# Attention with a memory and a gated expert on one core: products of ones at the start, beta spread by TensorE, a scaling pass folded, second score products of 64 rows

## The chip, the cores and the metric

The kernel runs on one core of a Trainium2 chip. The metric is the device time of one execution in microseconds, as the median of several runs; lower is better. Engines are named as in the profile: PE is TensorE, PEld its loading of weights, DVE is VectorE, ACT is ScalarE, POOL is GpSimd, SP is SyncE, which issues nearly all transfers here.

## The reference

There are 4 batches, 8 heads, 576 positions and 64 features a head. Each head has causal attention and a retrieval from a memory matrix; a gate made of beta mixes the two; a gated expert follows over all 2304 positions of width 512, with 1536 hidden columns.

```python
scores = scale * np.matmul(q, k.transpose(0, 1, 3, 2))
scores = np.where(causal, -1000000000.0, scores)
a = np.exp(scores - scores.max(-1, keepdims=True))
a /= a.sum(-1, keepdims=True) + 1e-09
local = np.matmul(a, v)
mem_ret = np.einsum('bhsd,bhde->bhse', q_p, M_prev)
mem_norm = np.einsum('bhsd,bhd->bhs', q_p, z_prev)[..., None] + 1e-06
g = 1.0 / (1.0 + np.exp(-beta))[None, :, None, None]
attn = g * mem_ret / mem_norm + (1 - g) * local
x = attn.transpose(0, 2, 1, 3).reshape(B * S, H * D)
out = ((1 / (1 + np.exp(-(x @ w_gate)))) * (x @ w_val)) @ w_out
```

Here q_p is phi(q), which is q + 1 for positive q and exp(q) otherwise.

## The kernel before

**Work and stages.** The 2304 rows are cut into six groups of 384: four groups hold the first 384 positions of a batch, two tail groups hold the last 192 positions of two batches each. The first group that is run is a tail group, the last one too. A group has four pairs of heads (24 pairs in all, numbered n from 0). A pair has three chunks c of 128 queries; each chunk gives scores for two heads j, which lie in the two halves of the 128 partitions. In a group of 384 the three chunks see 128, 256 and 384 keys. In a tail group two chunks see 512 keys, and the third, with 64 rows of either batch, sees 576 in two parts. After a chunk's scores VectorE adds the mask and finds the row's extreme (`scores`, L597), ScalarE takes the exponential (L606), the result is turned (`turn`) and multiplied with the values (`values`), scaled by `scaled`, and added to the memory's part (`memory`, scaled too). `scaled` divides by the sum in column D of the product and multiplies with the gate: gs for the memory, ga for the attention, both made by `gates` from beta.

**The expert.** `moe` goes over 12 blocks of 128 hidden columns for each group. Its products (L315) are of the type fp32r, which takes one pass; each is made of three products of a high and a low part. The weights come as 64-bit numbers and are turned into high and low parts in the first group (`convert`).

**Two forms of scores.** For n below 9 (SPLIT), and for the 64-row chunks, `heads` (L560) multiplies plain fp32: for each head a product over 64 rows, the two heads in the two halves of the array. Its profile rows say 64\*128, or 64\*64 for the 64-row chunks, and a plain fp32 product is recorded as two parts. From n = 9 on, `split` makes tiles for fp32r: `kq`, whose 128 partitions hold the high part of one head's queries and keys and the low part of its keys beside another copy of the queries' high part, and `ql`, the low part of its queries. The score of one head is then a product over all of kq and a second one of ql with kq, both of 128 rows; half of ql is zero (`half` writes the zeros once, on GpSimd), so that the unwanted half of kq adds nothing.

**Order.** Every operation is recorded in `Program` with an engine, a cost, and what it reads and writes; `plan` orders the operations of each engine by their recorded places and by these costs, and `issue` tries 800 shifted variants of the order, judged by its own model, and emits the best. So a changed cost or a removed operation can move any row of any engine. PE, DVE, ACT, POOL and SP each run their rows in this order and wait at a row until what it needs is there. In the model a product before the time COLD counts one and a half times.

**Beta.** It is loaded by one transfer that repeats its 8 numbers on all 128 partitions, behind the first keys and a memory matrix on SP. The first products of the program are the first pair's `heads`, once the first kp tile is there.

Of the kernel before, what the change touches and what calls it, by code (L numbers as in the profile page):

```python
# [9 lines left out]
F32 = mybir.dt.float32  # L10
# [19 lines left out]

WHEN = (20, 36)

COLD = 8.0

START = 0.7

# [204 lines left out]
def tile_attention_memory_moe(  # L241
# [82 lines left out]
    def act(n, emit, r, w):  # L324
        pg.add("act", 0.09 + n / 1200.0, emit, r, w)
# [22 lines left out]
    idn = sb.tile([128, 128], F32, name="idn")  # L348
    mask = sb.tile([128, 512], F32, name="mask")
    mask2 = sb.tile([128, 256], F32, name="mask2")  # L350
    bt = sb.tile([128, H], F32, name="bt")
    gs = sb.tile([128, H], F32, name="gs")
    ga = sb.tile([128, H], F32, name="ga")

# [19 lines left out]
            ), ["mask2"], ["mask2"])  # L374

    def gates():
        act(H, lambda: nc.scalar.activation(out=bt, in_=bt, func=AF.Exp, scale=-1.0), ["bt"], ["bt"])
        dve(H, lambda: nc.vector.tensor_scalar(
            out=gs, in0=bt, scalar1=1.0, scalar2=None, op0=ALU.add), ["bt"], ["gs"])
        dve(H * 8, lambda: nc.vector.reciprocal(out=gs, in_=gs), ["gs"], ["gs"])  # L380
        dve(H, lambda: nc.vector.tensor_scalar(
            out=ga, in0=gs, scalar1=-1.0, scalar2=1.0, op0=ALU.mult, op1=ALU.add), ["gs"], ["ga"])

    def half(t, k):
        r = slice(64, 128) if k[1] == 0 else slice(0, 64)
        pool(GT, lambda: nc.gpsimd.memset(t[r].bitcast(F32), 0.0), [], [k + ("z",)], fast=True)

    def pad(t, k):
        pool(64, lambda: nc.gpsimd.memset(t[:, S:], 0.0), [], [k + ("pad",)])
# [17 lines left out]
    plain, turned = {"wide": 4 * DM, 0: None}, {"wide": 4 * DM, 1: None}  # L407
    kq_r = Ring("kq", [128, 2 * GT], F32R, 5,
                {0: (in_wr, "wr", 2), **{i + 1: (in_wt, "wt", i) for i in range(4)}})
    ql_r = Ring("ql", [128, GT], F32R, 2, init=half)  # L410
    a_r = Ring("a", [128, 640], F32, 6, init=pad)
    st_r = Ring("st", [128, 2], F32, 6)
    at_r = Ring("at", [128, 1280], F32, 4)
# [84 lines left out]
    def scaled(out, out_k, t, tk, ring, eps, gate, gate_k):  # L498

        r, rk = ring.take()  # L500
        dve(6, lambda: nc.vector.tensor_scalar(
            out=r, in0=t[:, :, :, D], scalar1=eps, scalar2=None, op0=ALU.add), [tk], [rk])
        dve(48, lambda: nc.vector.reciprocal(out=r, in_=r), [rk], [rk])
        tt(nc.vector, ALU.mult, r, r, gate.unsqueeze(1).to_broadcast([128, 3, 2]), 6, [rk, gate_k], [rk])
        tt(nc.vector, ALU.mult, out, t[:, :, :, :D], r.unsqueeze(3).to_broadcast([128, 3, 2, D]), GT,
           [tk, rk], out_k)

# [24 lines left out]
    def split(n):  # L532


        if n >= NP or n < SPLIT:
            return
        u = pairs[n]
        u.kq = [[], []]
        ql = [ql_r.take() for _ in range(2)]
        nq, nk = (128, 512) if u.tail else (GT, GT)  # L540
        qs, ks = slice(u.qa, u.qa + nq), slice(u.ka, u.ka + nk)
        used = slice(0, S + nq if u.tail else 2 * GT)
        for e, (kp, kk) in enumerate(u.kp):
            for j in range(2):
                kq, k = kq_r.take()
                h, l = slice(64 * j, 64 * j + 64), slice(64 - 64 * j, 128 - 64 * j)
                kh, kd, kl, kx = k + ("h",), k + ("d",), k + ("l",), ql[j][1] + (e,)
                copy(kq[h, used], kp[h, used], used.stop, [kk], [kh])
                copy(kq[l, qs], kp[h, qs], nq, [kk], [kd])
                sub(nc.vector, kq[l, ks], kp[h, ks], kq[h, ks].bitcast(F32), nk, [kk, kh], [kl])  # L550
                q = ql[j][0][:, e * nq:(e + 1) * nq]
                sub(nc.vector, q[h], kp[h, qs], kq[h, qs].bitcast(F32), nq, [kk, kh], [kx])
                u.kq[j].append((kq, [kh, kd, kl], q, [kx, ql[j][1] + ("z",)]))

    def heads(u, es, sp, js, k0, k1):

        for e, q, m0, m1 in es:
            kp, _ = u.kp[e]
            for j, r in enumerate(js):
                nc.tensor.matmul(  # L560
                    out=sp[j][0][m0:m1, :k1 - k0], lhsT=kp[r, u.qa + q:u.qa + q + m1 - m0],
                    rhs=kp[r, u.ka + k0:u.ka + k1], start=True, stop=True)

    def scores(n, c):

        u = pairs[n]
        q0, W = items_of(u.g)[c]
        pair = u.tail and c == 2
        js = [slice(64 * j, 64 * j + 64) for j in range(2)]
        if (n, c) == (HP, 0):  # L570
            a_r.n, a_r.at = 5, 0
        a = [a_r.take() for _ in js]
        st = [st_r.take() for _ in js]
        ns = [(0, 320), (320, W)] if pair else [(0, W)]
        def part(i, k0, k1):
            m = k1 - k0
            sp = [bank("att") for _ in js]
            if pair:
                es = [(0, 128, 0, 64), (1, 128, 64, 128)]
                mk, mk_k = (mask2[:, :m], "mask2") if i else (mask[:, :m], "mask")  # L580
            else:
                es = [(c if u.tail else 0, q0, 0, 128)]
                mk, mk_k = mask[:, 512 - W:], "mask"
            with pg.block():
                if n < SPLIT or pair:
                    pe(4 * m / 2385.0 + 0.3, lambda: heads(u, es, sp, js, k0, k1),
                       [u.kp[e][1] for e, *_ in es], [sp[j][1] for j in range(2)])
                for j in range(2) if n >= SPLIT and not pair else ():
                    for e, q, m1 in [(es[0][0], q0, 128)]:
                        kq, kk, ql, kx = u.kq[j][e]  # L590
                        keys = kq[:, u.ka + k0:u.ka + k1]
                        out, out_k = sp[j][0][:m1, :m], sp[j][1]
                        matmul(out, kq[:, u.qa + q:u.qa + q + m1], keys, m, kk, [out_k], True, False)
                        matmul(out, ql[:, q:q + m1], keys, m, kk + kx, [out_k], False, True)
            for j in range(2):
                (aj, ak), (sj, sk), (pj, pk) = a[j], st[j], sp[j]
                dve(m + 60, lambda aj=aj, sj=sj, pj=pj: nc.vector.tensor_tensor_reduce(  # L597
                    out=aj[:, k0:k1], in0=pj[:, :m], in1=mk, scale=-0.125,
                    scalar=3.0e38 if i == 0 else sj[:, i - 1:i],
                    op0=ALU.add, op1=ALU.min, accum_out=sj[:, i:i + 1],  # L600
                ), [pk, mk_k] + [sk] * (i > 0), [ak, sk])

        for i, (k0, k1) in enumerate(ns):
            part(i, k0, k1)
        for (aj, ak), (sj, sk) in zip(a, st):
            act(W + 120, lambda aj=aj, sj=sj: nc.scalar.activation(  # L606
                out=aj[:, :W], in_=aj[:, :W], func=AF.Exp, scale=-1.0, bias=sj[:, len(ns) - 1:len(ns)],
            ), [ak, sk], [ak])
        u.a[c] = a
# [107 lines left out]
    def attn():  # L717
# [3 lines left out]
        load_pair(1)  # L721
        feature(0)
        load_values(0)
        load(bt, beta.unsqueeze(0).to_broadcast([128, H]), 500, [], ["bt"])
        pg.part = "attention"
        load_values(1)
        late = []
# [167 lines left out]
    def step():  # L895
# [2 lines left out]
        pg.part = "expert"  # L898
        return y

    constants()
    a = attn()
    done = 0
# [81 lines left out]
```

## Time and profile before

| | us |
|---|---|
| median of 3 runs (634.5 to 637.46) | 636.98 |
| the profiled execution | 639.4 |
| its span, from the first to the last instruction | 637.6 |
| PE busy | 620.8 (97%) |
| PEld busy | 547.2 (86%) |
| DVE busy | 427.7 (67%) |
| ACT busy | 301.9 (47%) |
| POOL busy | 9.2 (1%) |

The busy time of PE counts overlapping records once, and the end of a product is modelled, so a busy PE is not a PE at its peak; for the cost of a product one takes the distance between starts. In the chain that ended last PE has 78% of the span, transfers 10%, VectorE 6% and ScalarE 4%.

### The profile page before, as it was taken

How to read it: one execution, taken by the hardware profiler on the slowest of the kernel's cores; microseconds unless marked ns; L12 is line 12 of the kernel's file. 1: busy time of each engine (PE TensorE's matmuls, PEld its weight loads, DVE VectorE, ACT ScalarE, POOL GpSimd, SP SyncE). 2: the span in 40 equal slices, each digit the busy share in tenths (PEclk: the TensorE clock that was granted, in tenths of full speed). 3: DMA queues.
4: the chain of work that ended last, by engine and by line, in shares of the span. 5: the costliest groups of instructions: out<-in, count | busy, mean ns of one | idle time of the engine just before them, and what ended most of it. 6: DMA issues, size and time to landing. Idle time of an engine off the chain costs nothing.

```text
span 637.6 us, 12197 instructions
## 1 busy us (share of the span) xinstructions
PE 620.8 (97%) x4740; PEld 547.2 (86%) x4740; DVE 427.7 (67%) x1164; ACT 301.9 (47%) x589; POOL 9.2 (1%) x51
## 2 busy tenths in 40 slices
PE   7989999999999989999999999999999999999997
PEld 3658888888999888899999999989898989999996
DVE  5799999999966767778767786779797422111211
ACT  5988677757743433534534643536353231221111
POOL 2000000000000000000000000000000000000000
PEclk9999999999999989999999999999999999999999
DMA  8567789895599988559867467779588433134442
GB/s 301 193 221 229 241 285 329 293 311 171 152 269 275 225 128 209 112 154 266 204 187 222 118 168 214 169 207 253 142 163 205 140 134 132 67 116 159 171 174 74
DMA packets 94362, 124.04 MB, mean 195 GB/s; under 512 B 70881, under 2 KB 72929, under 8 KB 87009
## 3 DMA queue, kind: packets, MB, share of 16 engines
q1 hardware_dynamic: 94160, 123.01, 67.8%
q8 instruction: 37, 0.61, 0.4%
q10 hardware_dynamic: 144, 0.26, 0.1%
q14 instruction: 21, 0.16, 0.1%
HBM read 89.43 MB, written 17.30 MB: 167 GB/s over the span
## 4 chain that ended last, share of the span: by engine, by line
PE 78%; DMA 10%; DVE 6%; ACT 4%; issue 1%; DVEq 0%; ACTq 0%; SPq 0%
PE bank L315 65%; PE bank L319 7%; DMA tl_wr<-pl_wr 5%; DMA wr<-in_w_dram 5%; PE bank L560 3%; PE bank L322 2%; ACT a L606 1%; ACT at L328 1%; ACT wt L769 1%; DVE wt L776 1%; DVE a L597 1%; DVE wt L773 1%; DVE pl_wr L615 1%; DVE at L619 1%; DMA kp<-in_qk_dram 0%
## 5 line engine op out<-in xcount | busy, mean ns | idle before, releaser
L315 PE MATMUL bank<-xh,wg 128*128 128x384 f32 x576 | 167.0, 343 | 0.1
L315 PE MATMUL bank<-xh,sv 128*128 128x384 f32 x576 | 163.8, 341 | 1.1 <-DVE th_a L861 1.1
L315 PE MATMUL bank<-sv,gh 128*128 128x512 f32 x432 | 138.3, 398 | 0.0
L315 PEld LDWEIGHTS bank<-xh,wg 128*128 128x128 f32 x576 | 105.9, 189 | 5.5 <-issue 0.9
L315 PEld LDWEIGHTS bank<-xh,sv 128*128 128x128 f32 x576 | 105.8, 189 | 4.0 <-issue 1.8
L861 DVE SCALAR_TENSOR_TENSOR th_a<-th_a,bank 128x384 f32<-128x384 f32 x72 | 39.7, 552 | 100.7 <-PE bank L315 99.1
L606 ACT ACTIVATE a<-a,st 128x512 f32<-128x512 f32 (+3 forms) x144 | 80.2, 584 | 41.6 <-DVE st L597 40.9
L315 PE MATMUL bank<-xl,sv 128*128 128x384 f32 x288 | 98.1, 340 | 0.0
L315 PE MATMUL bank<-xl,wg 128*128 128x384 f32 x288 | 97.9, 340 | 0.0
L315 PEld LDWEIGHTS bank<-sv,gh 128*128 128x128 f32 x432 | 79.1, 188 | 13.3 <-issue 1.7
L328 ACT CAST gh<-th_a 128x384 fp32r<-128x384 f32 x72 | 36.9, 513 | 105.8 <-DVE th_a L861 105.6
L859 ACT ACTIVATE th_a<-bank 128x384 f32<-128x384 f32 x72 | 35.2, 489 | 107.4 <-PE bank L315 107.2
L315 PE MATMUL bank<-sv,gl 128*128 128x512 f32 x216 | 85.9, 399 | 0.0
L597 DVE CUSTOM_DVE_ANT_0 a<-bank,mask 128x128 f32<-128x128 f32 (+4 forms) x144 | 66.6, 484 | 18.0 <-PE bank L560 11.8
L619 DVE COPY at<-tl_wr 128x256 uint16<-128x256 uint16 (+3 forms) x90 | 46.0, 519 | 17.4 <-DMA tl_wr<-pl_wr 17.1
L315 PEld LDWEIGHTS bank<-xl,wg 128*128 128x128 f32 x288 | 54.4, 189 | 2.8 <-issue 0.3
L315 PEld LDWEIGHTS bank<-xl,sv 128*128 128x128 f32 x288 | 54.4, 189 | 0.2
L338 DVE TENSOR_TENSOR gl<-th_a,gh 128x384 fp32r<-128x384 f32 x72 | 39.9, 555 | 13.6 <-ACT gh L328 13.0
L315 PEld LDWEIGHTS bank<-sv,gl 128*128 128x128 f32 x216 | 40.6, 188 | 9.3 <-issue 0.5
L615 DVE COPY pl_wr<-a 128x256 uint16<-128x256 uint16 (+3 forms) x90 | 41.0, 471 | 4.8 <-DMA tl_wr<-pl_wr 3.0
L328 ACT CAST kq_wt<-kp 64x768 fp32r<-64x768 f32 (+3 forms) x60 | 36.9, 614 | 12.0 <-PE bank L315 10.8
L560 PE MATMUL bank<-kp 64*64 64x320 f32 (+5 forms) x220 | 33.6, 486 | 4.9 <-DMA kp<-in_qk_dram 3.9
(75 smaller groups left out, 700.5 us busy)
## 6 DMA issues: line engine op xcount, KB each, us to landing
sv<-w SPq DMA_DIRECT2D x45, 1024.0 KB, 5.1
wr<-in_w_dram SPq DMA_DIRECT2D x36, 512.0 KB, 4.7
kp<-in_qk_dram SPq DMA_DIRECT2D x32, 384.0 KB, 4.5
w<-sv SPq DMA_DIRECT2D x12, 1024.0 KB, 7.3
out_dram<-ob SPq DMA_DIRECT2D x14, 256.0 KB, 2.4
vt<-in_vp_dram SPq DMA_DIRECT2D x8, 330.0 KB, 3.9
vr<-in_vp_dram SPq DMA_DIRECT2D x8, 330.0 KB, 4.5
mb<-in_mz_dram SPq DMA_DIRECT2D x8, 260.0 KB, 4.2
```

Source lines behind the costliest of these rows:

```text
L315: lambda: nc.tensor.matmul(out=out, lhsT=lhsT, rhs=rhs, start=start, stop=stop), r, w)
L319: lambda: nc.tensor.matmul(out=out, lhsT=lhsT, rhs=rhs, start=start, stop=stop), r, w)
L322: pe(0.110, lambda: nc.tensor.transpose(out=out, in_=in_, identity=identity), r, w)
L328: act(n, lambda: nc.scalar.copy(out=out, in_=in_), r, w)
L338: dve(n, lambda: nc.vector.tensor_tensor(out=out, in0=in0, in1=in1, op=op), r, w)
L560: nc.tensor.matmul(out=sp[j][0][m0:m1, :k1 - k0], lhsT=kp[r, u.qa + q:u.qa + q + m1 - m0], rhs=kp[r, u.ka + k0:u.ka + k1], start=True, sto ...
L597: dve(m + 60, lambda aj=aj, sj=sj, pj=pj: nc.vector.tensor_tensor_reduce(out=aj[:, k0:k1], in0=pj[:, :m], in1=mk, scale=-0.125, scalar=3.0 ...
L606: act(W + 120, lambda aj=aj, sj=sj: nc.scalar.activation(out=aj[:, :W], in_=aj[:, :W], func=AF.Exp, scale=-1.0, bias=sj[:, len(ns) - 1:len ...
L615: dve(2 * W, lambda: nc.vector.tensor_copy(out=pl.rearrange("p (two w) -> p two w", two=2), in_=src), r, [pk], fast=True)
L619: dve(2 * W, lambda: nc.vector.tensor_copy(out=dst, in_=tl.rearrange("p (two w) -> p two w", two=2)), [lk], [key], fast=True)
L859: act(GT, lambda: nc.scalar.activation(out=th, in_=pg_[:, :GT], func=AF.Tanh, scale=0.5), [pg_k], [th_k])
L861: dve(GT, lambda: nc.vector.scalar_tensor_tensor(out=th, in0=th, scalar=1.0, in1=pv[:, :GT], op0=ALU.add, op1=ALU.mult,), [th_k, pv_k], [t ...
```

## The change

Five things are done. (1) `warm` has VectorE write a tile of ones, and TensorE multiplies it with itself seven times before anything else. (2) Beta is loaded to one partition; a product of a row of ones with it spreads it over the 128 partitions in a PSUM bank, from where ScalarE takes two exponentials. gs is now 1 + exp(-beta) and ga 1 + exp(beta), the reciprocals of what they were. (3) `scaled` therefore adds eps and multiplies with the gate in one VectorE instruction, takes the reciprocal, and has no third small pass. (4) The second score products read 64 rows: ql of both heads shares one tile, no half is zeroed, and `lows` issues the two heads' products one behind the other, each in its own half of the array. (5) In the planner's model COLD is 5.5, beta's transfer 4 KB, and the pair in `lows` has a cost of its own.

```diff
--- before.py
+++ after.py
@@ -30,7 +30,7 @@
 
 WHEN = (20, 36)
 
-COLD = 8.0
+COLD = 5.5
 
 START = 0.7
 
@@ -348,7 +348,8 @@
     idn = sb.tile([128, 128], F32, name="idn")
     mask = sb.tile([128, 512], F32, name="mask")
     mask2 = sb.tile([128, 256], F32, name="mask2")
-    bt = sb.tile([128, H], F32, name="bt")
+    bt = sb.tile([1, H], F32, name="bt")
+    ones = []
     gs = sb.tile([128, H], F32, name="gs")
     ga = sb.tile([128, H], F32, name="ga")
 
@@ -374,16 +375,25 @@
             ), ["mask2"], ["mask2"])
 
     def gates():
-        act(H, lambda: nc.scalar.activation(out=bt, in_=bt, func=AF.Exp, scale=-1.0), ["bt"], ["bt"])
-        dve(H, lambda: nc.vector.tensor_scalar(
-            out=gs, in0=bt, scalar1=1.0, scalar2=None, op0=ALU.add), ["bt"], ["gs"])
-        dve(H * 8, lambda: nc.vector.reciprocal(out=gs, in_=gs), ["gs"], ["gs"])
-        dve(H, lambda: nc.vector.tensor_scalar(
-            out=ga, in0=gs, scalar1=-1.0, scalar2=1.0, op0=ALU.mult, op1=ALU.add), ["gs"], ["ga"])
-
-    def half(t, k):
-        r = slice(64, 128) if k[1] == 0 else slice(0, 64)
-        pool(GT, lambda: nc.gpsimd.memset(t[r].bitcast(F32), 0.0), [], [k + ("z",)], fast=True)
+
+        b, bk = bank("att")
+        one, one_k = ones.pop()
+        product(b[:, :H], one, bt, H, [one_k, "bt"], [bk], True, True)
+        for t, sign in ((gs, -1.0), (ga, 1.0)):
+            k = "gs" if t is gs else "ga"
+            act(H, lambda t=t, sign=sign: nc.scalar.activation(out=t, in_=b[:, :H], func=AF.Exp, scale=sign), [bk], [k])
+            dve(H, lambda t=t: nc.vector.tensor_scalar(
+                out=t, in0=t, scalar1=1.0, scalar2=None, op0=ALU.add), [k], [k])
+
+    def warm():
+
+        z, zk = ob_r.take()
+        z = z[:, :128]
+        dve(128, lambda: nc.vector.memset(z, 1.0), [], [zk], fast=True)
+        ones.append((z[:1], zk))
+        t, tk = banks[7][0], pg.renew(banks[7][1])
+        for _ in range(7):
+            product(t[:, :128], z, z, 128, [zk], [tk], True, True)
 
     def pad(t, k):
         pool(64, lambda: nc.gpsimd.memset(t[:, S:], 0.0), [], [k + ("pad",)])
@@ -407,7 +417,7 @@
     plain, turned = {"wide": 4 * DM, 0: None}, {"wide": 4 * DM, 1: None}
     kq_r = Ring("kq", [128, 2 * GT], F32R, 5,
                 {0: (in_wr, "wr", 2), **{i + 1: (in_wt, "wt", i) for i in range(4)}})
-    ql_r = Ring("ql", [128, GT], F32R, 2, init=half)
+    ql_r = Ring("ql", [128, GT], F32R, 2)
     a_r = Ring("a", [128, 640], F32, 6, init=pad)
     st_r = Ring("st", [128, 2], F32, 6)
     at_r = Ring("at", [128, 1280], F32, 4)
@@ -498,10 +508,10 @@
     def scaled(out, out_k, t, tk, ring, eps, gate, gate_k):
 
         r, rk = ring.take()
-        dve(6, lambda: nc.vector.tensor_scalar(
-            out=r, in0=t[:, :, :, D], scalar1=eps, scalar2=None, op0=ALU.add), [tk], [rk])
+        dve(6, lambda: nc.vector.scalar_tensor_tensor(
+            out=r, in0=t[:, :, :, D], scalar=eps, in1=gate.unsqueeze(1).to_broadcast([128, 3, 2]),
+            op0=ALU.add, op1=ALU.mult), [tk, gate_k], [rk])
         dve(48, lambda: nc.vector.reciprocal(out=r, in_=r), [rk], [rk])
-        tt(nc.vector, ALU.mult, r, r, gate.unsqueeze(1).to_broadcast([128, 3, 2]), 6, [rk, gate_k], [rk])
         tt(nc.vector, ALU.mult, out, t[:, :, :, :D], r.unsqueeze(3).to_broadcast([128, 3, 2, D]), GT,
            [tk, rk], out_k)
 
@@ -536,7 +546,7 @@
             return
         u = pairs[n]
         u.kq = [[], []]
-        ql = [ql_r.take() for _ in range(2)]
+        ql, ql_k = ql_r.take()
         nq, nk = (128, 512) if u.tail else (GT, GT)
         qs, ks = slice(u.qa, u.qa + nq), slice(u.ka, u.ka + nk)
         used = slice(0, S + nq if u.tail else 2 * GT)
@@ -544,13 +554,13 @@
             for j in range(2):
                 kq, k = kq_r.take()
                 h, l = slice(64 * j, 64 * j + 64), slice(64 - 64 * j, 128 - 64 * j)
-                kh, kd, kl, kx = k + ("h",), k + ("d",), k + ("l",), ql[j][1] + (e,)
+                kh, kd, kl, kx = k + ("h",), k + ("d",), k + ("l",), ql_k + (j, e)
                 copy(kq[h, used], kp[h, used], used.stop, [kk], [kh])
                 copy(kq[l, qs], kp[h, qs], nq, [kk], [kd])
                 sub(nc.vector, kq[l, ks], kp[h, ks], kq[h, ks].bitcast(F32), nk, [kk, kh], [kl])
-                q = ql[j][0][:, e * nq:(e + 1) * nq]
-                sub(nc.vector, q[h], kp[h, qs], kq[h, qs].bitcast(F32), nq, [kk, kh], [kx])
-                u.kq[j].append((kq, [kh, kd, kl], q, [kx, ql[j][1] + ("z",)]))
+                q = ql[h, e * nq:(e + 1) * nq]
+                sub(nc.vector, q, kp[h, qs], kq[h, qs].bitcast(F32), nq, [kk, kh], [kx])
+                u.kq[j].append((kq, [kh, kd, kl], q, kx))
 
     def heads(u, es, sp, js, k0, k1):
 
@@ -560,6 +570,11 @@
                 nc.tensor.matmul(
                     out=sp[j][0][m0:m1, :k1 - k0], lhsT=kp[r, u.qa + q:u.qa + q + m1 - m0],
                     rhs=kp[r, u.ka + k0:u.ka + k1], start=True, stop=True)
+
+    def lows(parts, js, q, k0, k1):
+
+        for ((kq, _, ql, _), out, _), r in zip(parts, js):
+            nc.tensor.matmul(out=out, lhsT=ql[:, q:q + 128], rhs=kq[r, k0:k1], start=False, stop=True)
 
     def scores(n, c):
 
@@ -585,13 +600,14 @@
                 if n < SPLIT or pair:
                     pe(4 * m / 2385.0 + 0.3, lambda: heads(u, es, sp, js, k0, k1),
                        [u.kp[e][1] for e, *_ in es], [sp[j][1] for j in range(2)])
-                for j in range(2) if n >= SPLIT and not pair else ():
-                    for e, q, m1 in [(es[0][0], q0, 128)]:
-                        kq, kk, ql, kx = u.kq[j][e]
-                        keys = kq[:, u.ka + k0:u.ka + k1]
-                        out, out_k = sp[j][0][:m1, :m], sp[j][1]
-                        matmul(out, kq[:, u.qa + q:u.qa + q + m1], keys, m, kk, [out_k], True, False)
-                        matmul(out, ql[:, q:q + m1], keys, m, kk + kx, [out_k], False, True)
+                if n >= SPLIT and not pair:
+                    e, q, *_ = es[0]
+                    parts = [(u.kq[j][e], sp[j][0][:, :m], sp[j][1]) for j in range(2)]
+                    for (kq, kk, *_), out, out_k in parts:
+                        matmul(out, kq[:, u.qa + q:u.qa + q + 128], kq[:, u.ka + k0:u.ka + k1], m, kk, [out_k],
+                               True, False)
+                    pe(0.03 + m / 2210.0, lambda: lows(parts, js, q, u.ka + k0, u.ka + k1),
+                       [x for p in parts for x in (p[0][1][0], p[0][3])], [p[2] for p in parts])
             for j in range(2):
                 (aj, ak), (sj, sk), (pj, pk) = a[j], st[j], sp[j]
                 dve(m + 60, lambda aj=aj, sj=sj, pj=pj: nc.vector.tensor_tensor_reduce(
@@ -721,7 +737,7 @@
         load_pair(1)
         feature(0)
         load_values(0)
-        load(bt, beta.unsqueeze(0).to_broadcast([128, H]), 500, [], ["bt"])
+        load(bt, beta.unsqueeze(0), 4, [], ["bt"])
         pg.part = "attention"
         load_values(1)
         late = []
@@ -898,6 +914,7 @@
         pg.part = "expert"
         return y
 
+    warm()
     constants()
     a = attn()
     done = 0
```

On TensorE, at the start of the program, the rows of before are these (bank0 to bank7 are the PSUM banks, kp0 and kp1 the first pair's keys and queries of two batches, a0 an exponential that is turned):

```order
L560 MATMUL bank0_63<-kp0_101 128x512
L560 MATMUL bank1_64<-kp0_101 128x512
L560 MATMUL bank3_66<-kp1_102 128x512
L560 MATMUL bank4_67<-kp1_102 128x512
L560 MATMUL bank5_68<-kp0_101 64x320
L560 MATMUL bank6_69<-kp0_101 64x320
L560 MATMUL bank5_68<-kp1_102 64x320
L560 MATMUL bank6_69<-kp1_102 64x320
L322 MATMUL bank1_64<-idn_71,a0_112 128x128 x3
L560 MATMUL bank7_70<-kp0_101 64x256
```

and those of the changed kernel are these (ob0 is the tile of ones, bt is beta):

```order
L319 MATMUL bank7_70<-ob0_101 128x128 x7
L570 MATMUL bank0_63<-kp0_102 128x512
L570 MATMUL bank1_64<-kp0_102 128x512
L570 MATMUL bank4_67<-kp1_103 128x512
L570 MATMUL bank5_68<-kp1_103 128x512
L319 MATMUL bank2_65<-bt_74,ob0_101 128x8
L570 MATMUL bank6_69<-kp0_102 64x320
L570 MATMUL bank7_70<-kp0_102 64x320
L570 MATMUL bank6_69<-kp1_103 64x320
```

The products of ones and that of beta are new, and beta's stands ahead of the blocks of 64x320.

On TensorE, in the middle of the program, the second score products of pair 9 are between products of the expert in before (kq_wr2 is the kq tile of one head, kq_wt0 that of the other, sv and gh belong to the expert, mb and ph to the memory):

```order
L315 MATMUL bank7_70<-kq_wr2_160 128x128
L319 MATMUL bank6_69<-mb1_106,ph1_126 128x130
L315 MATMUL bank2_65<-sv1_146,gh0_151 128x512
L315 MATMUL bank7_70<-kq_wr2_160,ql0_158 128x128
L315 MATMUL bank2_65<-sv1_146,gl0_152 128x512
L315 MATMUL bank0_63<-sv1_146,gh0_151 128x512 x2
L315 MATMUL bank5_68<-kq_wt0_161 128x128
L315 MATMUL bank0_63<-sv1_146,gl0_152 128x512
L315 MATMUL bank5_68<-kq_wt0_161,ql1_159 128x128
L315 MATMUL bank1_64<-sv1_146,gh0_151 128x512 x2
```

In the changed kernel the pair of the same chunk stands so:

```order
L315 MATMUL bank5_68<-kq_wr2_160 128x128
L315 MATMUL bank3_66<-xh0_135,wg11_100 128x384
L315 MATMUL bank3_66<-xl0_136,wg11_100 128x384
L315 MATMUL bank3_66<-xh0_135,wg11_100 128x384
L315 MATMUL bank4_67<-xh0_135,sv2_154 128x384
L577 MATMUL bank5_68<-kq_wr2_160,ql0_159 128x128
L577 MATMUL bank6_69<-kq_wt0_161,ql0_159 128x128
L315 MATMUL bank4_67<-xl0_136,sv2_154 128x384
L315 MATMUL bank4_67<-xh0_135,sv2_154 128x384 x2
L315 MATMUL bank4_67<-xl0_136,sv2_154 128x384
```

The two heads' second products (L577) now stand behind each other, with 128-row products of the expert (L315) on both sides.

On VectorE, the first scaling of the memory's part in before (rn0 is the factor, xm0 the result; the ISA rows are the mask passes):

```order
L501 TENSOR_SCALAR rn0_117<-bank2_65 128x6
L503 RECIPROCAL rn0_117<-rn0_117 128x6
L597 ISA a0_112,st0_114<-bank3_66,mask_72 128x512
L597 ISA st0_114 128x1
L338 TENSOR_TENSOR rn0_117<-rn0_117,gs_75 128x6
L338 TENSOR_TENSOR xm0_116<-bank2_65,rn0_117 128x384
```

and in the changed kernel:

```order
L511 SCALAR_TENSOR_TENSOR rn0_118<-bank3_66,gs_75 128x6
L613 ISA a5_124,st5_126<-bank1_64,mask2_73,st5_126 128x256
L613 ISA st5_126 128x1
L514 RECIPROCAL rn0_118<-rn0_118 128x6
L504 SCALAR_TENSOR_TENSOR ph1_127<-kp2_104,ph1_127 128x192
L338 TENSOR_TENSOR xm0_117<-bank3_66,rn0_118 128x384
```

The multiplication of rn0 with gs is gone, and the first pass reads gs instead.

## Rows read from the trace of the kernel before

**Rows 1.** Busy time by stretch: engines, granted clock, DMA share, GB/s.

```profile
3.90:9.70 5.80, 5.77 (x19) 1.94 (x19) 2.39 (x8) 2.75 (x6) 0.59 (x2) 1.00 0.80 275
16.00:80.00 64.00, 60.28 (x772) 46.28 (x770) 57.51 (x176) 52.67 (x106) 1.01 (x9) 1.00 0.68 222
200.00:260.00 60.00, 56.65 (x420) 51.49 (x419) 42.21 (x128) 25.06 (x50) 1.10 (x3) 0.97 0.97 184
260.00:529.00 269.00, 268.86 (x2147) 242.61 (x2147) 192.40 (x522) 117.03 (x229) 2.59 (x12) 1.00 0.68 179
```

**Rows 2.** The chain that ended last, in order of time: start, length, what.

```profile
3.93 5.06 PE bank L560 x16
```

**Rows 3.** Instructions that read tile ql on PE: count, duration, starts, forms.

```profile
L315 PE MATMUL bank<-kq_wt,ql x64: 220/284/498, 163.3 to 506.8; 128*128 128x128 f32 x17, 128*128 128x384 f32 x17, 128*128 128x256 f32 x17, 128*128 128x512 f32 x13
...
L315 PE MATMUL bank<-kq_wr,ql x18: 222/282/396, 162.1 to 489.2; 128*128 128x128 f32 x5, 128*128 128x256 f32 x5, 128*128 128x384 f32 x5, 128*128 128x512 f32 x3
```

**Rows 4.** PE in order of time around two L560 blocks: start, duration, operation.

```profile
101.18 0.34 PE L315 MATMUL bank<-xl,sv 128*128 128x384 f32 x1
101.45 0.49 PE L560 MATMUL bank<-kp 64*128 64x128 f32 x4
101.87 0.62 PE L315 MATMUL bank<-xh,sv 128*128 128x384 f32 x2
102.33 0.34 PE L315 MATMUL bank<-xl,sv 128*128 128x384 f32 x1
...
151.41 0.34 PE L315 MATMUL bank<-xl,sv 128*128 128x384 f32 x1
151.58 0.34 PE L315 MATMUL bank<-xh,sv 128*128 128x384 f32 x1
151.85 0.92 PE L560 MATMUL bank<-kp 64*128 64x384 f32 x4
152.70 0.45 PE L315 MATMUL bank<-xh,sv 128*128 128x384 f32 x1
152.98 0.34 PE L315 MATMUL bank<-xl,sv 128*128 128x384 f32 x1
```

**Rows 5.** PE in order of time: products of ql and the next.

```profile
271.04 0.28 PE L315 MATMUL bank<-kq_wt,ql 128*128 128x128 f32 x1
271.15 0.39 PE L315 MATMUL bank<-xl,sv 128*128 128x384 f32 x1
...
422.02 0.40 PE L315 MATMUL bank<-kq_wt,ql 128*128 128x512 f32 x1
422.25 0.40 PE L315 MATMUL bank<-kq_wr 128*128 128x512 f32 x1
```

**Rows 6.** PE in order of time: plain fp32 products over 128 rows.

```profile
269.33 0.88 PE L319 MATMUL bank<-mb,ph 128*128 128x130 f32 x6
269.96 0.42 PE L315 MATMUL bank<-xl,wg 128*128 128x384 f32 x1
```

**Rows 7.** PE in order of time: three transposes between fp32r products.

```profile
421.10 0.34 PE L315 MATMUL bank<-xh,wg 128*128 128x384 f32 x1
421.28 0.49 PE L322 MATMUL bank<-idn,xs 128*128 128x128 f32 x3
...
421.79 0.39 PE L315 MATMUL bank<-kq_wt 128*128 128x512 f32 x1
```

**Rows 8.** PE in order of time: L560 blocks later in the start.

```profile
9.72 0.45 PE L560 MATMUL bank<-kp 64*64 64x256 f32 x4
...
14.73 1.13 PE L560 MATMUL bank<-kp 64*128 64x512 f32 x4
...
18.10 0.77 PE L560 MATMUL bank<-kp 64*64 64x320 f32 x8
```

**Rows 9.** ACT in order of time, with the wait before beta's exponential.

```profile
8.92 0.21 ACT L377 ACTIVATE bt<-bt 128x8 f32<-128x8 f32 x1 [1.30 <-DMA bt<-in_beta_dram]
```

**Rows 10.** Instructions of tile rs on DVE: count, ns min/median/max, starts.

```profile
L338 DVE TENSOR_TENSOR rs<-rs,ga x24: 155/166/167, 24.4 to 524.6; 128x6 f32<-128x6 f32 x24
```

## The prediction

> **What bounds the kernel now.** I read the table by stretches first [rows 1]. From 260 to 529 us TensorE is busy 268.86 of 269 us while VectorE has 192.40 and ScalarE 117.03, so there every microsecond that TensorE gains or loses moves the end. The reader should look at the two other stretches as well: from 16 to 80 us TensorE is busy 60.28 of 64 and VectorE 57.51, so the attention of the first group is nearly as tight on both, and from 200 to 260 us TensorE stands idle for 3.35 us of 60. That idle time is the only cover that extra TensorE work finds after 80 us. The chain of waits tells the start: it goes through the first keys' products from 3.93 us on [rows 2].
>
> Busy time is not enough for costs, since neighbouring products overlap in the records. So I take prices from starts in the order of time: the distance from one product's start to the next one's start.
>
> **The second score products, before.** The tile ql is read by 64 + 18 = 82 products, 22 each of 128, 384 and 256 keys and 16 of 512 [rows 3]. A product of 384 columns is followed by the next after 0.17 us (151.41 to 151.58) [rows 4]; I use 0.175, which is also what three in a row give. The ql product of 128 keys takes 0.11 us (271.04 to 271.15), that of 512 takes 0.23 (422.02 to 422.25) [rows 5]. For 256 I take 0.455 ns a column, as for 384 and 512, so 0.117 us. The sum is 22 x (0.11 + 0.117 + 0.175) + 16 x 0.23 = 8.8 + 3.7 = 12.5 us.
>
> **And after.** The two heads' ql products become two 64-row products behind each other, 33 pairs in the groups of 384 queries and 8 in the last tail group, 41 in all. No row shows a 64-row product of this number type. The nearest is the older form of the scores, L560: the same two row halves, 64 rows by 128 columns, between the same 128-row products. Three of its features can be read in [rows 4]. With 384 keys it stands between products that start at 151.58 and 152.98: 1.40 us, less two products of 0.175, makes 1.05 for the block. With 128 keys, 101.18 to 102.33 holds three L315 products: 1.15 - 0.525 = 0.625. So the block costs 0.625 + (1.05 - 0.625) = 1.05 for 256 columns more, 1.66 ns a column, and at no columns 0.625 - 128 x 0.00166 = 0.41 us is left. The slope is four cycles at 2.4 GHz, while each of the block's four recorded parts alone takes two cycles a column (a 130-column part takes 0.11 us: six of them from 269.33 to 269.96 [rows 6]); so the two halves do run side by side. The 0.41 us is the price of leaving 128 rows and coming back. It isn't the number type: three transposes, of the same plain type as L560 but 128 rows, fit in from 421.10 to 421.79 = 0.69 us, of which two products make 0.35 (the second one starts between) and three transposes the other 0.34 [rows 7].
>
> The Trainium skill ("TensorEngine Tiling (Array Packing)", section Key Properties) says that changing the tiling mode, not just the tile, drains TensorE; it speaks against this edit, and the rows agree: the block of 64 rows starts 0.27 us after the product before it, where 0.17 is usual.
>
> So a new pair costs 0.41 us and its stream. The stream at 0.455 ns a column is 0.058, 0.117, 0.175 and 0.233 us: 11 x 0.35 + 8 x 0.233 = 5.7 us. With 41 x 0.41 = 16.8 us that is 22.5 us, **10.0 us more** than the 12.5 before. From below the fixed part can be nothing (the halves side by side, at once), which makes the edit 12.5 - 5.7 = 6.8 us cheaper. I take 0.41, since block, neighbours and place are the same and only the number type and the second pass differ. Cover: the ql products are spread from 163 to 507 us [rows 3], so about a sixth of the pairs, 7 at 0.24 us, falls in 200 to 260 us, where TensorE waits anyway; I take 1 us off (bounds 0 and 1.7).
>
> **The ones at the start.** VectorE writes them as its first work, so TensorE can begin at about 1.1 us (my assumption; no row shows VectorE that early). A product with 128 columns of this type is two recorded parts of 0.11 us at full speed [rows 6], seven are 1.5 us and at half speed 3.0; they end at about 4.1, when the keys, at 3.93, have just landed. What they may buy: the first blocks take 5.06 us from 3.93 [rows 2], though a block of 512 keys takes 1.13 later and the 320-key one 0.77: two and one make 3.0 us [rows 8]. That is nearer the pace of 1.2 GHz, though the granted clock stands at 1.00 of 2.4 GHz for that stretch [rows 1]. From 9.72 on the records are short (0.45 us for four parts of 256 columns), 5.8 us after the first product. If the full pace comes as late after the first product of ones, it is there at 6.9, and half of the 2.8 us up to 9.7 is saved: 1.4, less some 0.4 for products of ones that end late. I take **-1.0**; bounds +0.4 (no earlier) and -2.0 (full pace for all keys).
>
> **Beta.** ScalarE waited 1.30 us for beta's transfer, with the second head's exponential queued behind [rows 9]. Now one row is landed instead of 128, and the exponential stands ahead of the gates. I take **-0.7**, bounds 0 and -1.3. The risk is new: the product that spreads beta stands on TensorE ahead of the 320-key blocks, so these wait for beta. TensorE comes to it at about 7.7 us (3.93 and the 512-key blocks' three quarters of 5.06); did beta land as late as before, at 8.92, it would lose 1.2 us.
>
> **VectorE.** 48 scalings lose a multiplication of 0.166 us, and the fused pass, on the same six elements, is priced as the one that it replaces [rows 10]: 48 x 0.166 = 8.0 us of VectorE, hidden where TensorE is the bound. Perhaps ten of them, those of five pairs, stand in the first 80 us, where VectorE is busy 57.51 of 64 [rows 1]: **-0.5**, bounds 0 and -1.7. The zeroing of ql leaves an idle GpSimd: nothing. With one ql tile a pair instead of two, a tile is free one pair earlier, which loosens a wait that TensorE doesn't see.
>
> **Sum.** +10.0 - 1.0 - 1.0 - 0.7 - 0.5 = +6.8 us on the profiled execution's 639.4 (637.6 span and 1.8 around it), 646.2. The median of the runs shown, 636.98, lies 2.4 lower: **643.8**. The planner also rewrites nearly every row of the order; its luck is worth a microsecond or two either way and is in the ranges.
>
> **Rivals.** *Side by side without a fixed cost* ends on the other side: pairs at 5.7 us give -6.8, with -2.2 from the start and VectorE, 628.0. For it speaks that the halves overlap fully in L560 and that its four parts hide loads of weights; against it, the 0.41 us that is the same for 128 and 384 keys. It decides the sign when the fixed part falls below (12.5 - 5.7 + 2.2) / 41 = 0.22 us. The Trainium skill ("TensorE: Matmul & The Clock Gate", section Measured speedup vs the span model) gives such a pack as one product and about 4 ns a tile more, with no word of the change of mode; the rows agree for the block's inside alone. *Half the fixed cost*: if part of 0.41 belongs to the second pass that only the plain type has, some 0.2 stays: 41 x 0.2 + 5.7 - 12.5 = +1.4, with -2.2, 636.2. *Late beta* adds 1.2 to any of them (645.0 to the forecast).
>
> **Chances.** The fixed cost applies: 0.55, its own range 640 to 648. No fixed cost: 0.27. Half of it: 0.18. The range of 627 to 648 leaves out a part of the second below and little of the first above. A change of 0.5%, 3.2 us, is about what a measurement can tell from none. Faster takes 0.27 and a fifth of the half case: 0.31. The same takes most of the half case and the low end of the first: 0.16. Slower is left with 0.53.
>
> **What would show it.** In the trace after, the distance from the last 128-row product before a 64-row pair to the second one behind it shows the fixed part at once: 0.41 us over the streams, or nothing. TensorE should be at its full pace by 7 us, and the stretch to 80 us be a little shorter. I am wrong if the pairs fit in without a gap, or if the planner's new order opens idle time on TensorE after 80 us.

## The result and the profile after

The changed kernel takes 644.93 us (median of 4 runs, 643.89 to 646.47), the kernel before 635.74 us beside it (4 runs, 634.17 to 637.46): a ratio of 1.0146, 95% interval 1.0107 to 1.0185. It is slower by 9.2 us. The profiled execution took 646.47 us with a span of 644.6.

The first view is again the table by stretches, with the columns of [rows 1]: PE, PEld, DVE, ACT and POOL busy, granted clock, DMA share, GB/s. The line above the dots is from the kernel before, the others are from the changed one.

```profile
160.00:200.00 40.00, 40.00 (x257) 36.51 (x256) 30.71 (x91) 21.83 (x42) 0.11 (x1) 1.00 0.84 240
...
16.00:80.00 64.00, 59.55 (x758) 44.27 (x756) 59.77 (x173) 52.73 (x107) 1.20 (x9) 1.00 0.72 243
160.00:200.00 40.00, 37.79 (x238) 33.33 (x237) 27.32 (x78) 16.29 (x33) 0.11 (x1) 0.96 0.77 224
200.00:260.00 60.00, 60.00 (x442) 53.47 (x438) 45.39 (x128) 26.50 (x52) 0.39 (x3) 1.00 0.86 206
260.00:537.00 277.00, 276.91 (x2162) 242.22 (x2161) 190.29 (x499) 118.49 (x231) 1.59 (x12) 1.00 0.65 171
```

TensorE is still the bound after 200 us: it is busy 60.00 of 60 and 276.91 of 277 us. The idle 3.35 us of before between 200 and 260 us [rows 1] are gone, but from 160 to 200 us, where TensorE had no idle time before, it now has 2.21 us; nearly all of that is one wait of 1.96 us for VectorE (PE in order of time, the wait in brackets):

```profile
178.62 0.44 PE L315 MATMUL bank<-kq_wr 128*128 128x384 f32 x1 [1.96 <-DVE xs L338]
```

So most of the idle time has moved. From 16 to 80 us TensorE is a little less busy than before, VectorE a little more.

The next view holds the 64-row products of tile ql on PE: count, shortest/median/longest record, first and last start, forms. They are 82 as before [rows 3], now on 64 rows, and spread over the same part of the program.

```profile
L577 PE MATMUL bank<-kq_wt,ql x64: 322/386/498, 161.7 to 513.1; 64*128 64x128 f32 x17, 64*128 64x256 f32 x17, 64*128 64x384 f32 x17, 64*128 64x512 f32 x13
...
L577 PE MATMUL bank<-kq_wr,ql x18: 323/384/492, 161.7 to 495.7; 64*128 64x128 f32 x5, 64*128 64x256 f32 x5, 64*128 64x384 f32 x5, 64*128 64x512 f32 x3
```

Two of the pairs, on PE in order of time (start, record's duration, operation), with what stands around them:

```profile
227.84 0.22 PE L315 MATMUL bank<-kq_wt 128*128 128x128 f32 x1
227.99 0.33 PE L577 MATMUL bank<-kq_wt,ql 64*128 64x128 f32 x2
228.25 0.44 PE L315 MATMUL bank<-xl,wg 128*128 128x384 f32 x1
228.53 0.34 PE L315 MATMUL bank<-xh,wg 128*128 128x384 f32 x1
...
249.32 0.34 PE L315 MATMUL bank<-kq_wt 128*128 128x384 f32 x1
249.59 0.45 PE L577 MATMUL bank<-kq_wt,ql 64*128 64x384 f32 x2
249.97 0.50 PE L315 MATMUL bank<-sv,gh 128*128 128x512 f32 x1
250.31 0.40 PE L315 MATMUL bank<-sv,gl 128*128 128x512 f32 x1
```

The reader reads the cost of a pair as in [rows 4], from the start of the 128-row product ahead of it to the start of the second one behind it. With 384 keys that is 250.31 - 249.32 = 0.99 us. The product ahead takes 0.175 and the one behind, of 512 columns, 0.23, so the pair costs 0.58; its stream is 0.175, and 0.41 us is left. With 128 keys it is 0.69 - 0.058 - 0.175 = 0.46, less a stream of 0.058: 0.40 us. So both halves run in the time of one stream, and each pair pays about the 0.41 us that the plain fp32 block paid before, whatever its length. Read in the same way, the 31 pairs of this trace that stand between L315 products have a median of 0.395 us, and the medians of the four lengths lie between 0.389 and 0.399.

The loads of weights around the pair of 384 keys show where this time goes (PEld in order of time):

```profile
249.10 0.19 PEld L315 LDWEIGHTS bank<-kq_wt 128*128 128x128 f32 x1
249.59 0.19 PEld L577 LDWEIGHTS bank<-kq_wt,ql 64*128 64x128 f32 x2 [0.30 <-issue]
249.97 0.19 PEld L315 LDWEIGHTS bank<-sv,gh 128*128 128x128 f32 x1 [0.19 <-issue]
250.07 0.19 PEld L315 LDWEIGHTS bank<-sv,gl 128*128 128x128 f32 x1
```

The load for the 128-row product at 249.32 runs at 249.10, beside the product ahead of it. The pair's loads start only at 249.59, with the pair itself, and the load for the 128-row product behind it only at 249.97, as that product starts. So neither change of rows has its load of weights ahead of time.

The start of the program on PE in order of time, with the idle time ahead and what ended it in brackets:

```profile
1.05 3.35 PE L319 MATMUL bank<-ob 128*128 128x128 f32 x14 [1.05 <-DVE ob L392]
4.33 2.44 PE L570 MATMUL bank<-kp 64*128 64x512 f32 x8
6.70 0.38 PE L319 MATMUL bank<-bt,ob 1*128 1x8 f32 x2
7.01 0.77 PE L570 MATMUL bank<-kp 64*64 64x320 f32 x8
...
9.53 0.63 PE L322 MATMUL bank<-idn,a 128*128 128x128 f32 x4 [0.73 <-ACT a L622]
```

The products of ones begin at 1.05 us and the keys' follow at 4.33. The two 512-key blocks take 2.44 us and the 320-key one 0.77, close to the pace of later ones (twice 1.13, and 0.77) [rows 8], where before all three took 5.06 [rows 2]. Beta has landed when its product's turn comes, and ScalarE no longer waits 1.30 us for it [rows 9]. Then, at 9.53 us, TensorE stands 0.73 us for ScalarE's exponential; in the trace of experiment 9, the same kernel, the same transposes start at 8.89 us without a wait. A scaling's fused pass takes 164 ns, as long as the multiplication that is gone (166) [rows 10].

```profile
L511 DVE SCALAR_TENSOR_TENSOR rs<-bank,ga x24: 148/164/165, 23.5 to 530.9; 128x6 f32<-128x6 f32 x24
```

VectorE tells how far the start has come. Its first mask pass over 320 keys, first before, then in the changed kernel:

```profile
10.53 0.48 DVE L597 CUSTOM_DVE_ANT_0 a<-bank,mask 128x320 f32<-128x320 f32 x1
...
9.21 0.49 DVE L613 CUSTOM_DVE_ANT_0 a<-bank,mask 128x320 f32<-128x320 f32 x1
```

It starts 1.3 us earlier.

### The profile page after: what moved, and what is told of

It reads as the page before. It is cut to its first block, busy times and chain, and to the rows that moved or that the text cites. A ratio compares the mean times of both kernels' runs of the same rounds, so it can differ in the third digit from the quotient of the medians.

```text
span 644.6 us, 12185 instructions
## 1 busy us (share of the span) xinstructions
PE 631.3 (98%) x4756; PEld 547.4 (85%) x4756; DVE 425.2 (66%) x1116; ACT 300.1 (47%) x590; POOL 6.8 (1%) x49
## 4 chain that ended last, share of the span: by engine, by line
PE 80%; DVE 9%; DMA 6%; ACT 2%; issue 1%; SPq 1%; DVEq 0%; ACTq 0%
PE bank L315 65%; PE bank L319 8%; DMA wr<-in_w_dram 4%; PE bank L322 3%; PE bank L570 2%; PE bank L577 2%; DMA tl_wr<-pl_wr 2%; DVE a L613 1%; DVE wt L789 1%; DMA kp<-in_qk_dram 1%; DVE wt L792 1%; DVE at L635 1%; ACT wt L785 1%; DVE pl_wr L631 1%; DVE sv L338 1%
## 5 line engine op out<-in xcount | busy, mean ns | idle before, releaser
L315 PE MATMUL bank<-xh,wg 128*128 128x384 f32 x576 | 168.6, 345 | 0.0
L315 PE MATMUL bank<-xh,sv 128*128 128x384 f32 x576 | 163.0, 341 | 0.0
L315 PE MATMUL bank<-sv,gh 128*128 128x512 f32 x432 | 141.4, 403 | 0.0
L315 PEld LDWEIGHTS bank<-xh,wg 128*128 128x128 f32 x576 | 106.0, 189 | 5.7 <-issue 1.2
L315 PEld LDWEIGHTS bank<-xh,sv 128*128 128x128 f32 x576 | 105.5, 189 | 1.9 <-DVE at L635 0.5
L315 PE MATMUL bank<-xl,wg 128*128 128x384 f32 x288 | 98.3, 341 | 0.0
L315 PE MATMUL bank<-xl,sv 128*128 128x384 f32 x288 | 98.0, 340 | 0.0
L622 ACT ACTIVATE a<-a,st 128x512 f32<-128x512 f32 (+2 forms) x144 | 79.0, 581 | 31.4 <-DVE st L613 30.3
L315 PEld LDWEIGHTS bank<-sv,gh 128*128 128x128 f32 x432 | 78.2, 188 | 17.2 <-issue 4.6
L315 PE MATMUL bank<-sv,gl 128*128 128x512 f32 x216 | 86.0, 398 | 0.0
L613 DVE CUSTOM_DVE_ANT_0 a<-bank,mask 128x512 f32<-128x512 f32 (+2 forms) x144 | 66.3, 487 | 20.8 <-PE bank L570 10.3
L315 PEld LDWEIGHTS bank<-xl,wg 128*128 128x128 f32 x288 | 54.6, 189 | 4.0 <-issue 1.4
L315 PEld LDWEIGHTS bank<-xl,sv 128*128 128x128 f32 x288 | 54.4, 189 | 1.8 <-issue 1.7
L315 PEld LDWEIGHTS bank<-sv,gl 128*128 128x128 f32 x216 | 40.6, 188 | 8.9 <-issue 0.3
L322 PE MATMUL bank<-idn,a 128*128 128x128 f32 x184 | 30.5, 284 | 5.0 <-ACT at L328 2.6
```

What stands on the lines that cost most here:

```text
L315: lambda: nc.tensor.matmul(out=out, lhsT=lhsT, rhs=rhs, start=start, stop=stop), r, w)
L322: pe(0.110, lambda: nc.tensor.transpose(out=out, in_=in_, identity=identity), r, w)
L622: act(W + 120, lambda aj=aj, sj=sj: nc.scalar.activation(out=aj[:, :W], in_=aj[:, :W], func=AF.Exp, scale=-1.0, bias=sj[:, len(ns) - 1:len ...
```

## The experiments

All times are medians; "before" is the kernel before, measured along with each experiment. Experiments 1, 2, 5, 6 and 7 keep the changed kernel's order of rows and change only what an operation issues; experiment 9 is the changed kernel itself, and the others are planned anew. Three dots mark what is left out of a diff.

**1. The second products on 128 rows, same order.** This isolates the pairs from the order.

```diff
...
-            nc.tensor.matmul(out=out, lhsT=ql[:, q:q + 128], rhs=kq[r, k0:k1], start=False, stop=True)
+            nc.tensor.matmul(out=out, lhsT=ql[:, q:q + 128], rhs=kq[:, k0:k1], start=False, stop=True)
```

> The changed kernel row for row, only that the second score products read 128 rows of the shared ql tile again (this adds the other head's low part to each score, so the output isn't the reference's). Theory of the fixed cost: 41 pairs give back 0.24 us each, 9.9 us, so 635 us. Rival, that the new order of rows costs the time and the pairs don't: 645 us, no change.

Measured: 635.48 us (before 635.54; ratio 0.9993, 0.9971 to 1.0015). A pair of 384 keys on PE in order of time, with the product behind it:

```profile
219.39 0.34 PE L577 MATMUL bank<-kq_wt,ql 128*128 128x384 f32 x1
219.57 0.34 PE L577 MATMUL bank<-kq_wr,ql 128*128 128x384 f32 x1
219.75 0.40 PE L315 MATMUL bank<-sv,gh 128*128 128x512 f32 x1
```

and the stretches that have idle time now and had it before:

```profile
160.00:200.00 40.00, 37.76 (x285) 34.68 (x284) 28.84 (x81) 15.63 (x32) 0.12 (x2) 1.00 0.87 241
200.00:260.00 60.00, 60.00 (x452) 55.97 (x451) 45.83 (x133) 26.43 (x54) 0.69 (x4) 1.00 0.82 204
```

The two 128-row products take 0.36 us together, where the 64-row pair takes 0.58, and 9.2 us are gone against the changed kernel's 644.64 in experiment 9 (by the ratios to before, 9.0 us against experiment 9 and 9.7 against the first result). The pairs cost the whole loss; the order of rows and the other edits together cost nothing. TensorE is idle for 2.24 us from 160 to 200 us and not at all from 200 to 260, as with the pairs (2.21 and none), so the moved gap belongs to the new order and is not cover that the pairs used.

**2. Two changes of rows for each pair, same order.** The second head's 128-row product is issued between the two 64-row ones.

```diff
...
+            if j == 1:
+                second()
             nc.tensor.matmul(out=out, lhsT=ql[:, q:q + 128], rhs=kq[r, k0:k1], start=False, stop=True)
...
```

> The changed kernel row for row, only that the second head's 128-row product is issued between the two 64-row products, so that TensorE leaves 128 rows twice for each pair. Theory of the fixed cost: 41 x 0.41 us more, and 5.7 us more of streams that no longer overlap, about 22 us: 667 us. Rival, that the cost is not paid per change of rows: the streams alone, 651 us.

Measured: 664.71 us (before 635.54; ratio 1.0467, 1.0439 to 1.0496), 20 us over the changed kernel. On PE in order of time (L609 is the 128-row product):

```profile
250.73 0.34 PE L609 MATMUL bank<-kq_wt 128*128 128x384 f32 x1
251.00 0.44 PE L579 MATMUL bank<-kq_wt,ql 64*128 64x384 f32 x1
251.37 0.44 PE L609 MATMUL bank<-kq_wt 128*128 128x384 f32 x1
251.74 0.44 PE L579 MATMUL bank<-kq_wt,ql 64*128 64x384 f32 x1
252.11 0.50 PE L315 MATMUL bank<-sv,gh 128*128 128x512 f32 x1
252.45 0.40 PE L315 MATMUL bank<-sv,gl 128*128 128x512 f32 x1
```

From 250.73 to 252.45 are 1.72 us. Four streams of 0.175 and one of 0.23 make 0.93, and 0.79 is left, 0.40 for each of the two times that TensorE leaves 128 rows and comes back. The cost is paid each time, as the theory says. By the ratios to before the total is 20.4 to 21.1 us; what is missing to its 22 is no more than these measurements can tell.

**3. The other edits alone.** The changed kernel with the score products of before.

```diff
-    ql_r = Ring("ql", [128, GT], F32R, 2)
+    ql_r = Ring("ql", [128, GT], F32R, 2, init=half)
...
-                    pe(0.03 + m / 2210.0, lambda: lows(parts, js, q, u.ka + k0, u.ka + k1),
+                        matmul(out, ql[:, q:q + m1], keys, m, kk + kx, [out_k], False, True)
...
```

> The changed kernel with the score products of before (128 rows, half of ql zero): ones, beta by TensorE and the folded scaling alone, planned anew. The prediction's terms for these: 2.2 us less than before, 633.5 us. Rival, from the trace of the changed kernel, where the 100th product of the expert starts 2.7 us later than in before: the start brings nothing or a loss, 636 to 639 us.

Measured: 633.79 us (before 635.54; ratio 0.9975, 0.9952 to 0.9997). It is the fastest median of the study, but the interval ends near one; experiment 10 asks again.

**4. The 64-row products alone**, in the kernel before.

```diff
...
-                        matmul(out, ql[:, q:q + m1], keys, m, kk + kx, [out_k], False, True)
+                    pe(0.03 + m / 2210.0, lambda: lows(parts, js, q, u.ka + k0, u.ka + k1),
...
```

> The kernel before with the 64-row score products alone, planned anew. Theory of the fixed cost: 10 us less 1 us of cover, 645 us. Halves side by side without a fixed cost: 629 us. Rival, that the loss comes with the other edits: 636 us.

Measured: 646.17 us (before 635.54; ratio 1.0158, 1.0124 to 1.0191). The loss comes with this edit alone.

**5. No products of ones, same order.** VectorE's writing of the ones stays.

```diff
-            product(t[:, :128], z, z, 128, [zk], [tk], True, True)
+            pe(4 * 128 / 2385.0, lambda: None, [zk], [tk])
```

> The changed kernel row for row without its seven products of ones. Theory of the prediction: they are worth about 1.0 us (bounds 0 and 2), so 645.9 us. Rival: TensorE gets ahead only to wait for VectorE and ScalarE in the first 16 us, 644.9 us, no change.

Measured: 646.39 us (before 635.46; ratio 1.0164, 1.0137 to 1.0192). PE in order of time:

```profile
4.18 3.79 PE L570 MATMUL bank<-kp 64*128 64x512 f32 x8 [4.18 <-DMA kp<-in_qk_dram]
7.89 0.59 PE L319 MATMUL bank<-bt,ob 1*128 1x8 f32 x2
8.41 1.23 PE L570 MATMUL bank<-kp 64*64 64x320 f32 x8
```

Without the ones the same blocks take 3.79 us for 2.44 and 1.23 for 0.77, and beta's product comes 1.2 us later. So the ones do bring the full pace earlier. ScalarE's first exponentials over 576 keys, at the same place of the order, start at 20.33 us here, and at 19.42, 18.60 and 19.47 us in the traces of the changed kernel, experiment 9 and experiment 7, so 0.9 to 1.7 us are still there at 20 us. On the whole time it is 1.75 us against experiment 9 and 1.71 against experiment 7, which was measured beside it, but the ratios' intervals (1.0137 to 1.0192, 1.0108 to 1.0161 and 1.0118 to 1.0189) overlap: a gain is likely, its size isn't settled.

**6. Beta landed on 128 partitions again, same order.**

```diff
...
-        load(bt, beta.unsqueeze(0), 4, [], ["bt"])
+        load(bt, beta.unsqueeze(0).to_broadcast([128, H]), 4, [], ["bt"])
```

> The changed kernel row for row, only that beta's transfer writes 128 partitions again, of which the product reads one. The product of beta then waits until about 8.9 us and TensorE stands in front of the 320-key blocks. Theory: 1 to 2 us more, 646 to 647 us. Rival: the wait is hidden by later waits of the start, 644.9 us.

Measured: 646.69 us (before 635.46; ratio 1.0172, 1.0145 to 1.0200), 2 us over experiment 9. PE in order of time:

```profile
8.77 0.38 PE L319 MATMUL bank<-bt,ob 1*128 1x8 f32 x2 [1.77 <-DMA bt<-in_beta_dram]
9.08 1.31 PE L570 MATMUL bank<-kp 64*64 64x320 f32 x8
```

The wait of the rival "late beta" is there, 1.77 us; and the block behind it takes 1.31 us, where it took 0.77 with one row of beta: after the idle time TensorE is back at the slow pace. ScalarE's exponentials over 576 keys start at 22.07 us, 2.6 to 3.5 us later than in the three traces named in experiment 5. That the single row is what keeps beta's product from waiting is shown; the effect on the whole time is at the edge of what these measurements can tell.

**7. Three small passes in each scaling, same order.**

```diff
-        dve(6, lambda: nc.vector.scalar_tensor_tensor(
-            out=r, in0=t[:, :, :, D], scalar=eps, in1=gate.unsqueeze(1).to_broadcast([128, 3, 2]),
-            op0=ALU.add, op1=ALU.mult), [tk, gate_k], [rk])
...
+            nc.vector.tensor_scalar(out=r, in0=t[:, :, :, D], scalar1=eps, scalar2=None, op0=ALU.add)
+            nc.vector.tensor_tensor(out=r, in0=r, in1=gate.unsqueeze(1).to_broadcast([128, 3, 2]), op=ALU.mult)
...
```

> The changed kernel row for row, only that each of the 48 scalings has its third small pass on VectorE again (8 us of VectorE). Theory of the prediction: 0.5 us more, 645.4 us, since most lies beside TensorE's work. Rival, that VectorE sets the pace of the first 160 us: 1.5 to 3 us more, 646.5 to 648 us.

Measured: 644.68 us (before 635.46; ratio 1.0154, 1.0118 to 1.0189), the changed kernel's own time. VectorE does carry 48 passes more; tile rs alone has

```profile
L512 DVE TENSOR_SCALAR rs<-bank x24: 149/164/166, 23.6 to 528.6; 128x6 f32<-128x6 f32 x24
L513 DVE TENSOR_TENSOR rs<-rs,ga x24: 166/166/170, 23.8 to 528.8; 128x6 f32<-128x6 f32 x24
```

and nothing of the 8 us can be seen in the time. An effect of 0.5 us can't be told from none here, since the interval is 4.5 us wide.

**8. Another seed of the planner's search, kernel before.**

```diff
-        pick = random.Random(1)
+        pick = random.Random(2)
```

> The kernel before with another seed of the planner's random search, nothing else. If the order is worth a microsecond or two either way, 633.5 to 637.5 us; if 640 or more, the difference between any two planned kernels here is mostly luck of the order.

Measured: 635.58 us (before 635.46; ratio 0.9996, 0.9974 to 1.0018). With this second order the kernel before takes the same time.

**9. The changed kernel once more.**

> The changed kernel itself once more, as a yardstick for the small edits: 644 to 646 us if the numbers of the products of ones (1.5 us) and of beta's transfer (1.8 us) are effects; 646 us or more if they are the spread between takings.

Measured: 644.64 us (before 636.27; ratio 1.0135, 1.0108 to 1.0161). It agrees with the first result, 1.0146.

**10. Experiment 3 with another seed**, the edit as in 8.

> The start edits and the folded scaling with the score products of before, with another seed of the planner's search. If these edits are worth 1 to 2 us whatever the order, 633.5 to 634.5 us; if the 1.75 us measured with the first seed was luck of the order, 635.5 us.

Measured: 636.46 us (before 636.27; ratio 1.0006, 0.9985 to 1.0026). With this order the other edits bring nothing that can be measured. The same edits gave 1.75 us less with the first seed, so either an order is worth that much, or part of it is the spread between measurements.

## Why the prediction was right

**The pairs.** This is the step that decided, and it held in kind and size. The fixed part read from two L560 blocks, 0.41 us, was 0.40 and 0.41 us in the two pairs shown and 0.395 in the median, though their number type is another and they have no second pass; the halves overlap, as the slope of the old blocks said. The term was +10.0 us with 1.0 taken off for cover; experiment 1 against experiment 9 gives 9.2 on the same order of rows, and experiment 4 10.6 for this edit alone. Both rivals without the full fixed part fall with these rows and times, and with experiment 2, where the same products with one more change of rows a pair cost 20 us more. The Trainium skill's sentence that a change of tiling mode drains TensorE ("TensorEngine Tiling (Array Packing)", section Key Properties) agrees with the rows here: a pair of 384 keys starts 0.27 us after the product ahead, where 0.18 is usual. The Trainium skill gives no price there. The rows give one: 0.09 us of the 0.41 lie ahead of the pair, the rest between the pair's start and the next products' regular spacing, where the next load of weights starts only with its product.

**The cover.** 1.0 us was taken off because TensorE idled between 200 and 260 us. The reason was wrong: the new order moved most of this idle time to the wait that ends at 178.62 us, and there it is as long with the pairs as without them (experiment 1). The sum came near all the same, partly by luck: 41 pairs at 0.395 us instead of 0.41 are 0.6 us less, an estimate from the median, and the rest is within the spread of the measurements. The prediction named new idle time after 80 us as a sign that it was wrong. These 1.96 us are that, but before had 3.35 us at another place, and experiment 1 takes the time of before although it has this wait too.

**The start.** This term was mis-sized: -1.0 for the ones, -0.7 for beta and -0.5 for VectorE, together -2.2. In the changed kernel's order these edits together bring nothing that can be measured (experiment 1 is a ratio of 0.9993 to before), in another order 1.75 us (experiment 3), in a third none (experiment 10). Their steps happen as described: the full pace comes earlier, beta is there in time, the pass is gone. The full pace came sooner than assumed: from about 5.3 us on the parts of the 512-key blocks start 0.43 us apart instead of 0.85, where the prediction had 6.9 us. At 10 us VectorE is 1.3 us ahead of before, which is near the 1.7 forecast for ones and beta. So the terms were about right where they arise and wrong in what reaches the end. From 16 to 80 us TensorE is no busier than before. The VectorE part can't be seen (experiment 7), which doesn't tell 0.5 us from none. For the ones and beta's transfer experiments 5 and 6 make a gain in this order likely, 1.75 and 2.0 us, with intervals that overlap that of experiment 9. How that goes with the zero of all edits together was not settled: it would mean that the new order as a whole gives back what they bring.

**The sum.** The forecast was +6.8 us on a median of 637.0; it became +9.2 on a median of 635.74. Nearly all of the difference is the start term, which was counted and did not come; the lower median of before hid half of it in the absolute time, which is luck. The range, 627 to 648, also holds the times of the two rivals, 628.0 and 636.2, so it is the rows of the pairs and the experiments that show the mechanism, not that the time fell inside.

## What to carry to other kernels

In this kernel products on half the rows overlap well, but between 128-row products each excursion costs a fixed time, here 0.4 us; a pair that saves one stream of at most 0.23 us can't earn that back. Price an edit from the nearest block in the trace by fitting a line through two lengths: the slope says whether the halves overlap, and the rest is what each excursion costs. And an earlier start has to be followed to the end: here VectorE was 1.3 us ahead at 10 us, and the whole time shows it in one order of three at most.

## What the runs showed of the hardware

After 1.77 us of idle time at the start (experiment 6) TensorE's next block took 1.31 us instead of 0.77, and the pace stayed low for the blocks behind it. From 9.2 us on the granted clock is 0.50, the lower of the levels of 1.2 and 2.4 GHz (columns of the table by stretches):

```profile
9.20:12.50 3.30, 3.30 (x20) 1.34 (x21) 2.42 (x11) 3.01 (x8) 0.12 (x1) 0.50 1.04 410
```

By ScalarE's row at 22.07 us the wait has cost 2.6 us or more, against its own 1.77. Such a fall is not the same in every execution. In the changed kernel's trace and in that of experiment 7 TensorE waits 1.96 us for VectorE at the same place, and then, in that order:

```profile
179.50:182.50 3.00, 3.00 (x10) 3.00 (x11) 2.29 (x8) 2.05 (x5) 0.11 (x1) 0.50 1.02 282
...
179.50:182.50 3.00, 3.00 (x20) 2.80 (x20) 2.55 (x10) 2.88 (x6) 0.11 (x1) 1.00 1.02 308
```

In one the clock fell and 10 products are recorded in 3 us, in the other it didn't and there are 20.

The 1.00 that [rows 1] gives for 3.9 to 9.7 us is no measurement: that trace holds no record of the granted clock before 9.64 us. The pace of the products is the only sign there.

The changed kernel's executions had mean granted clocks of 0.994 to 0.999 for one and the same order, and spans from 644.6 to 641.8 us that roughly follow them: some of the spread between runs of this kernel is the clock.
